# Stationary columns of the chunk steps laid side by side, and their zero matmuls taken out

## The chip, the cores and the metric

The kernel runs on one core of one Trainium2 chip. The metric is the device time of one execution in microseconds (us). A core has TensorE (PE; its weight loads are shown apart as PEld), VectorE (DVE), ScalarE (ACT), GpSimd (POOL), and SyncE (SP), which here only issues transfers. All transfers run on 16 DMA engines. The clock granted to TensorE varies; the profile gives it as a share of full speed.

## The reference

Three stages follow each other: a recurrent attention with a state per head, a mixture of 8 experts with one expert per token, and a gated layer for all tokens. The change is in the first:

```python
B, H, S, D = (4, 8, 768, 48)
k_n = k / (norm(k) + 1e-06)
state = zeros((B, H, D, D))
for t in range(S):
    kt, vt, bt = (k_n[:, :, t], v[:, :, t], beta[:, :, t, None])
    y[:, :, t] = einsum('bhd,bhde->bhe', q[:, :, t], state)
    v_old = einsum('bhde,bhd->bhe', state, kt)
    state = state + bt[:, :, :, None] * einsum('bhd,bhe->bhde', kt, vt - v_old)
```

The output y, 3072 tokens of 384 numbers, goes into the experts (`_moe_ref`: argmax of a gate, two matrices with a ReLU between, scaling) and then into `sigmoid(x @ w_gate) * (x @ w_val) @ w_out`.

## The kernel before

**Chunks and steps.** The 768 tokens of a sequence are cut into 24 chunks of 32. One chunk step `s` does 32 tokens of all 4 batches and 8 heads: the 128 partitions hold 4 batches x 32 tokens. Steps are numbered 0 to 23; `g = s // 4` is the group of four steps, `u = s // 2` the pair of steps, `s2 = s % 2`. Within a chunk the recurrence is solved with the inverse of a 32x32 triangular matrix per batch and head, made for a whole group of four steps at a time.

**One step** (the loop over `s` that begins at line 758), with the names under which the profile shows its parts:

- `KS`: the keys (stationary `KB`) times the state `SH`, 32 matmuls. VectorE makes `W` from it and the values (line 789).
- `Y`, first part: the queries (`QB`) times the state, 32 matmuls. From step 19 on, 12 of these come later in the step.
- zero matmuls into unused columns of U's bank (line 813): 4 a step, 2 from step 19 on. `zf` is a tile of zeros; nobody reads their result.
- `U`: the inverse (`TBD`) times `W`, 32 matmuls. ScalarE rounds U to f16 (`UH[:, 0]`), VectorE takes the remainder (`UH[:, 1]`), so that two f16 halves stand for one f32.
- `XTP`: three transposes of the previous step's output rows, for the gate.
- `GP`: the products of keys with keys and queries of the step 11 chunks ahead, 24 matmuls, with 8 more at the end of the step. Steps 13 to 23 have none left; in their place stand 10 zero matmuls, 2 from step 19 on (line 842).
- `Sps`: the state's update, 48 matmuls (line 858): 2 batch pairs `p`, 3 passes over the f16 halves, 8 heads. The stationary operand is a slice of `KBD`. ScalarE copies the sum to `SH` for the next step.
- `Y`, second part: 24 matmuls (line 866) with a slice of `PBD` as the stationary operand, 3 passes and 8 heads. ScalarE copies Y out (`XG`).
- `GL`: the gate's logits, 12 matmuls.

Step 0 has no KS and no first part of Y; behind its Sps stand 16 more zero matmuls (`BP`, line 861), and ahead of the KS of step 1 stand 8 (`BURST`, line 785).

**KBD and PBD.** Both are block-diagonal over the batches, double-buffered by `u`, zeroed once, and refilled by transfers within SBUF. KBD holds the normalised keys by tokens in two f16 halves, `[128, s2, half, batch of the pair, 64, 8 heads]`: the columns of one head stand 8 elements, 16 bytes, apart. PBD holds the masked products of queries and keys in two f16 halves, `[128, half, 4 batches, 32 tokens x 16]`, where the 16 are 2 steps x 8 heads: the columns of one head stand 16 elements, 32 bytes, apart.

**What fills them.** For PBD: `gp_evac` (line 271) copies the query half of GP to `P` on ScalarE; `p_split` (284) scales and masks on GpSimd; `p_split_hi` and `p_split_lo` make the two halves `PHL`; `expand` (301) issues four transfers of 32 partitions each. For groups ahead of the loop `p_first` and `p_evac` (252, 265) do the same with the tile `PM`. For KBD: `load_kth` reads the keys to `kth`, `kh_mul` (306) scales them on ScalarE, `kh_split_hi` and `kh_split_lo` (316, 323) make the halves `KH` on ScalarE and GpSimd, and `kexp` (329) issues four transfers. In an even step `s`, `expand` and `kexp` for the next pair are issued behind the KS of that step; the tiles are first read two steps later.

**What sets the order.** Each engine's instructions in this stage go out in the order of the program text (class `Queue`, line 95 in the profile stands for all of them). VectorE's work on the next group's inverse is put between its W and UH by `Filler`, by fixed budgets a step (`TA`, `TB`); at the end of a group's fourth step what remains of it is issued in one go. All transfers named here are issued by SP, in program order.

Of the kernel before, what the change touches and what calls it, by code (L numbers as in the profile page):

```python
# [47 lines left out]
WG = 2.7  # L48
WP = 4.5
WE = 1.0  # L50
NU = 4
TC = 3.8
NR = 8
Q2 = 0.0
GS = 6
BURST = {1: 8}
BP = {0: 16}
KA = 1
SHE = (0, 32, 24, 20, 20, 20)
NP = 0  # L60
TA = 2.4
TB = 4.2
W0 = 36
# [15 lines left out]
RK = LA + 1
STROWS = 128  # L80
# [68 lines left out]
class Attention:  # L149
# [5 lines left out]
    def run(self, small, acc, zero_fill, small_loads):  # L155
        tc, a, beside = self.tc, self.a, self.beside
        nc = tc.nc
        V, A, G = [Queue(tc, e) for e in (nc.vector, nc.scalar, nc.gpsimd)]
        T, SP = Queue(tc, nc.tensor), Queue(tc, nc.sync)
        engines = (V, A, G, T, SP)  # L160
        ctx, early = ExitStack(), ExitStack()
        wk = ctx.enter_context(tc.tile_pool(name="at_w", bufs=1, side="right"))
        cp = ctx.enter_context(tc.tile_pool(name="at_c", bufs=1, side="right"))
# [4 lines left out]
        pp = ctx.enter_context(tc.tile_pool(name="at_p", bufs=1, space=PSUM))  # L168
# [9 lines left out]
        KB = [(ep if i < 8 else cp).tile([128, 2, 64, 8], F32, name=f"KB{i}") for i in range(RK)]  # L178
        QB = [cp.tile([128, 2, 64, 8], F32, name=f"QB{i}") for i in range(2)]
        TBD = [(cp if i else ep).tile([128, 2, 1024], F32, name=f"TBD{i}") for i in range(2)]  # L180
        PBD = [cp.tile([128, 2, 4, 512], F16, name=f"PBD{i}") for i in range(2)]
        KBD = [cp.tile([128, 2, 2, 2, 64, 8], F16, name=f"KBD{i}") for i in range(2)]
        Sps = [pp.tile([128, 512], F32, name=f"Sps{i}") for i in range(2)]
        KT, VT, KTOK, KHG, GPM, PHL, LT = {}, {}, {}, {}, {}, {}, {}

# [59 lines left out]
        QF, PM, PP = {}, {}, {}  # L245
# [6 lines left out]
        def p_first(s):  # L252

            u, s2 = divmod(s, 2)
            q = QF[s]
            if s2 == 0:
                PM[u] = wk.tile([128, 32, 16], F32, tag="PHL", name="PM", bufs=4)
            tag = ("GP", "XTP", "GL", "U")[s]
            ps = pool(tag).tile([128, 8, 64], F32, tag=tag, name="P0", bufs=1)
            for h in range(8):  # L260
                for p in range(2):
                    T.matmul(out=ps[64 * p : 64 * p + 64, h, 0:32], lhsT=KB[s][0:112, p, :, h], rhs=q[0:112, p, :, h], start=True, stop=True)
            PP[s] = ps

        def p_evac(s):
            u, s2 = divmod(s, 2)
            ps = PP.pop(s)
            for h in range(8):
                A.activation(out=PM[u][:, :, 8 * s2 + h], in_=ps[:, h, 0:32], func=AF.Copy, scale=rnt[:, 0, 8 * s + h : 8 * s + h + 1])

        def gp_evac(s):

            ps = GPS.pop(s)
            KT.pop(s)
            g, s4 = divmod(s, 4)
            if s4 == 0 and g > 0:
                GPM[g] = [ep.tile([128, 32, 32], F32, tag=n, name=n, bufs=b) for n, b in (("G", 2), ("P", 2))]
            A.copy(out=GPM[g][0][:, 8 * s4 : 8 * s4 + 8], in_=ps[:, :, 0:32])
            return A.copy(out=GPM[g][1][:, :, 8 * s4 : 8 * s4 + 8].rearrange("p i h -> p h i"), in_=ps[:, :, 32:64]).ins


        PMS = {}
# [1 line left out]
        def p_split(u):  # L284
            g, i = divmod(u, 2)
            if g:
                pm = GPM[g][1][:, :, 16 * i : 16 * i + 16]
                G.tensor_tensor(out=pm, in0=pm, in1=rnt[:, g, 16 * i : 16 * i + 16].unsqueeze(1).to_broadcast([128, 32, 16]), op=ALU.mult)
            else:
                pm = PM.pop(u)  # L290
            G.tensor_tensor(out=pm, in0=pm, in1=mask.unsqueeze(2).to_broadcast([128, 32, 16]), op=ALU.mult)
            PHL[u] = wk.tile([128, 2, 32, 16], F16, tag="PHL", name="PHL", bufs=4)
            PMS[u] = pm

        def p_split_hi(u):
# [4 lines left out]

        def expand(dst, src):
            for b in range(4):
                SP.dma_start(out=dst[32 * b : 32 * b + 32, :, b], in_=src[32 * b : 32 * b + 32].rearrange("p a i k -> p a (i k)"))


        def kh_mul(u, half=None):
            r = rnt[:, u // 2].rearrange("p (s h) -> p s h", s=4)
            for i in (range(2) if half is None else (half,)):
# [4 lines left out]
                    continue  # L313
                G.tensor_tensor(out=kt, in0=kt, in1=r[:, 2 * (u % 2) + i].unsqueeze(1).to_broadcast([128, 48, 8]), op=ALU.mult)

        def kh_split_hi(u):
            KH = wk.tile([128, 2, 2, 384], F16, tag="KH", name="KH", bufs=1)
            src = KTOK[u].rearrange("p s d h -> p s (d h)")
            for s in range(2):
                A.copy(out=KH[:, s, 0], in_=src[:, s])  # L320
            KHG[u] = KH

        def kh_split_lo(u):
            KH = KHG[u]
            src = KTOK.pop(u).rearrange("p s d h -> p s (d h)")
            for s in range(2):
                G.tensor_tensor(out=KH[:, s, 1], in0=src[:, s], in1=KH[:, s, 0], op=ALU.subtract)

        def kexp(u):
            KH = KHG.pop(u)  # L330
            for b in range(4):
                SP.dma_start(
                    out=KBD[u % 2][32 * b : 32 * b + 32, :, :, b % 2, 0:48].rearrange("p s a d h -> p (s a) (d h)"),
                    in_=KH[32 * b : 32 * b + 32].rearrange("p s a x -> p (s a) x"))


        def prep(g):
# [416 lines left out]
        mm = lambda **kw: T.matmul(skip_group_check=True, **kw)  # L754
# [3 lines left out]
        for s in range(NSTEP):  # L758
            g, s4 = divmod(s, 4)
# [22 lines left out]
            if s > 0:  # L782
                KSf = pp.tile([128, 512], F32, tag="KS", name="KS")
                KSp = KSf[:, 0:384].rearrange("p (h e) -> p h e", h=8)
                for _ in range(BURST.get(s, N1)):
                    mm(out=KSf[:, 384:512], lhsT=zf, rhs=zf, start=True, stop=True)
                for h, p, r in hp:
                    mm(out=KSp[r, h], lhsT=KB[s % RK][:, p, :, h], rhs=S0[:, p, 48 * h : 48 * h + 48], start=True, stop=True)
                V.scalar_tensor_tensor(out=W, in0=vp, scalar=SIG * KSC, in1=KSp, op0=ALU.mult, op1=ALU.subtract)
# [20 lines left out]
            if s == 0:  # L810
                for _ in range(B0):
                    mm(out=Uf[:, 384:512], lhsT=zl, rhs=zl, start=True, stop=True)
            for _ in range((NUL if s >= LS else NU) if s else 0):
                mm(out=Uf[:, 384:512], lhsT=zf, rhs=zf, start=True, stop=True)
            for h, p, r in hp:
                mm(out=Up[r, h], lhsT=TBD[g % 2][r].rearrange("p b k -> p (b k)")[:, 8 * s4 + h :: 32], rhs=W[r, h], start=True, stop=True)
            fil.run(TA if s else Q2)
# [714 lines left out]
```

## Time and profile before

| | |
|---|---|
| runs | 1119.1, 1122.11, 1122.72 us |
| median | 1122.11 us |
| the profiled execution | 1119.2 us, span 1117.5 us |
| instructions | 22890 |
| packets moved | 73535, 100.13 MB |
| mean granted clock | 0.862 |

The chunk steps take the stretch from about 62 to 392 us of the span; the experts follow to about 655 us, then the gated layer. The page shows busy time per engine, the span in 40 slices, DMA queues and groups of instructions. Nearly all instructions of the chunk steps carry line 95, the helper that records them, so they are read by the names of tiles: `Sps<-UH,KBD` is a matmul into Sps with UH and KBD as operands. Matmuls overlap: the duration of one reaches well beyond the start of the next, so that the cost of a group is read from start to start.

### The profile page before, as it was taken

How to read it: one execution, taken by the hardware profiler on the slowest of the kernel's cores; microseconds unless marked ns; L12 is line 12 of the kernel's file. 1: busy time of each engine (PE TensorE's matmuls, PEld its weight loads, DVE VectorE, ACT ScalarE, POOL GpSimd, SP SyncE). 2: the span in 40 equal slices, each digit the busy share in tenths (PEclk: the TensorE clock that was granted, in tenths of full speed). 3: DMA queues.
4: the chain of work that ended last, by engine and by line, in shares of the span. 5: the costliest groups of instructions: out<-in, count | busy, mean ns of one | idle time of the engine just before them, and what ended most of it. 6: DMA issues, size and time to landing. Idle time of an engine off the chain costs nothing. (4 is left out here: it accounts for less than half of the span.)

```text
span 1117.5 us, 22890 instructions
## 1 busy us (share of the span) xinstructions
PE 1086.5 (97%) x9287; PEld 986.8 (88%) x9288; DVE 552.1 (49%) x1376; ACT 412.5 (37%) x892; POOL 422.4 (38%) x460
## 2 busy tenths in 40 slices
PE   9899999999999999999989999999999999999997
PEld 8798999999999998888888988888888888888886
DVE  7977677877873357756767255430210201201111
ACT  6644545445444245454445422221211211211111
POOL 8544445544642123535544413432131221312312
PEclk8885556755556589999999999999999999999999
DMA  7986634432334336545553322100000000000000
GB/s 188 235 209 158 156 103 129 116 100 75 89 91 137 94 104 217 154 144 185 160 167 110 110 45 71 57 29 1 1 29 1 13 17 1 29 1 1 29 1 28
DMA packets 73535, 100.13 MB, mean 90 GB/s; under 512 B 9721, under 2 KB 62914, under 8 KB 73426
## 3 DMA queue, kind: packets, MB, share of 16 engines
q1 hardware_dynamic: 70354, 89.17, 29.1%
q0 software_dynamic: 3072, 9.46, 2.3%
q8 instruction: 74, 1.21, 0.5%
q14 instruction: 35, 0.29, 0.1%
HBM read 74.94 MB, written 15.80 MB: 81 GB/s over the span
## 5 line engine op out<-in xcount | busy, mean ns | idle before, releaser
L1453 DVE TENSOR_TENSOR gf<-gf,g 128x512 f32<-128x512 f32 x72 | 49.5, 688 | 308.7 <-PE g L1445 308.2
L954 POOL TENSOR_TENSOR gsl<-gf,gsh 128x512 fp32r<-128x512 f32 x68 | 88.4, 1301 | 268.0 <-ACT gsh L953 268.0
L1452 ACT ACTIVATE gf<-g 128x512 f32<-128x512 f32 x72 | 43.0, 597 | 183.4 <-PE g L1445 182.9
L953 ACT CAST gsh<-gf 128x512 fp32r<-128x512 f32 x69 | 42.8, 620 | 146.4 <-DVE gf L1453 146.0
L95 DVE TENSOR_TENSOR X<-X,tmp 128x60 f32<-128x60 f32 (+25 forms) x282 | 91.3, 349 | 1.2
L95 DVE TENSOR_TENSOR tmp<-X,Lt 128x60 f32<-128x60 f32 (+25 forms) x282 | 87.0, 335 | 1.9
L1419 PE MATMUL o<-woh,gsl 128*128 128x384 f32 x272 | 87.2, 338 | 0.0
L1419 PE MATMUL o<-wol,gsh 128*128 128x384 f32 x272 | 86.5, 337 | 0.0
L95 PE MATMUL Sps<-UH,KBD 64*128 64x48 f16 x1104 | 65.4, 228 | 2.6 <-DVE UH L95 2.6
L95 PEld LDWEIGHTS <-KBD 64*128 64x128 f16 x1104 | 62.7, 166 | 5.9 <-issue 4.2
L1134 DVE SCALAR_TENSOR_TENSOR hl<-h,hh 128x460 fp32r<-128x460 f32 (+7 forms) x57 | 33.1, 581 | 65.4 <-ACT hh L1133 65.1
L1445 PE MATMUL g<-yl,wgh 128*128 128x512 f32 x216 | 62.6, 395 | 0.0
L1093 PE MATMUL y<-hh,w2h 128*128 128x460 f32 (+6 forms) x168 | 61.0, 363 | 1.5 <-ACT hh L1133 1.4
L1445 PE MATMUL g<-yl,wvh 128*128 128x512 f32 x216 | 62.3, 395 | 0.0
L1419 PE MATMUL o<-woh,gsh 128*128 128x384 f32 x272 | 61.7, 337 | 0.0
L1445 PE MATMUL g<-yh,wgh 128*128 128x512 f32 x180 | 60.9, 395 | 0.0
L1093 PE MATMUL y<-hh,w2l 128*128 128x460 f32 (+6 forms) x168 | 58.9, 351 | 0.0
L95 ACT ACTIVATE kth<-kth,rnt 128x48 f32<-128x48 f32 x192 | 54.7, 375 | 6.6 <-DMA kth<-in_ktok_dram 6.4
L1419 PEld LDWEIGHTS o<-woh,gsh 128*128 128x128 f32 x272 | 49.7, 188 | 5.8
L95 PE MATMUL GP<-KT,KB 112*64 112x64 f32 x640 | 47.7, 315 | 5.8 <-DMA KB<-in_st_dram 3.7
L1071 POOL TENSOR_TENSOR w1l<-w1r,w1h 128x768 fp32r<-128x768 f32 x19 | 37.1, 1952 | 41.5 <-ACT w1h L1066 41.2
L1419 PEld LDWEIGHTS o<-wol,gsh 128*128 128x128 f32 x272 | 50.6, 188 | 2.4
(333 smaller groups left out, 2559.5 us busy)
## 6 DMA issues: line engine op xcount, KB each, us to landing
w1r<-in_w_dram SPq DMA_DIRECT2D x32, 384.0 KB
w2r<-in_w_dram SPq DMA_DIRECT2D x32, 384.0 KB
KT<-in_st_dram SPq DMA_DIRECT2D x20, 448.0 KB
disp<-TBD SPq DMA_DIRECT2D x8, 772.0 KB
kth<-in_ktok_dram SPq DMA_DIRECT2D x12, 384.0 KB
VT<-in_vtok_dram SPq DMA_DIRECT2D x12, 384.0 KB
KBD<-KH SPq DMA_DIRECT2D x48, 96.0 KB
XG<-in_m2g_dram SPq DMA_DIRECT2D x12, 384.0 KB
```

Source lines behind the costliest of these rows:

```text
L95: r = f(*args, **kw)
L953: (act or nc.scalar).copy(out=hi, in_=src)
L954: eng.tensor_tensor(out=lo, in0=src, in1=hi, op=ALU.subtract)
L1071: engine.tensor_tensor(out=l, in0=self.raw[b][i], in1=h, op=ALU.subtract)
L1093: self.T.matmul(out=ys[c][:, 0:n], lhsT=w2[l][:, f % 2, 128 * c : 128 * c + 128], rhs=(hh, hl)[r], start=(f == 0 and i == 0), stop=(f == 7 ...
L1134: self.V.scalar_tensor_tensor(out=hl, in0=hp[:, 0:n], scalar=0.0, in1=hh, op0=ALU.max, op1=ALU.subtract)
L1419: T.matmul(out=ops_[m][:, 0:384], lhsT=gh[l][:, 128 * m : 128 * m + 128], rhs=wo[r][:, f], start=(f == 0 and i == 0), stop=(f == 11 and i ...
L1445: T.matmul(out=ps, lhsT=gv[w][l][:, c, 128 * f : 128 * f + 128], rhs=Y[r][c], start=(i == 0 and c == 0), stop=(i == 2 and c == 2))
L1452: A.activation(out=gf, in_=gps[0], func=AF.Sigmoid)
L1453: V.tensor_tensor(out=gf, in0=gf, in1=gps[1], op=ALU.mult)
```

## The change

KBD becomes `[128, s2, half, 8 heads, 2 batches, 64]` and PBD `[128, half, 16, 4 batches, 32]`: the 128 columns of one head lie side by side. What feeds them follows: P, PM and PHL hold the 16 ahead of the 32 tokens, KH the heads ahead of the 48; the casts and subtractions of KH read `kth` through a view with heads first, and the copy from GP to P no longer turns the two. The transfers of `expand` and `kexp` place runs of 32 and of 48 f16 numbers. The zero matmuls of the chunk steps are left out, those ahead of the loop and in step 0 ahead of U stay.

```diff
-        PBD = [cp.tile([128, 2, 4, 512], F16, name=f"PBD{i}") for i in range(2)]
-        KBD = [cp.tile([128, 2, 2, 2, 64, 8], F16, name=f"KBD{i}") for i in range(2)]
+        PBD = [cp.tile([128, 2, 16, 4, 32], F16, name=f"PBD{i}") for i in range(2)]
+        KBD = [cp.tile([128, 2, 2, 8, 2, 64], F16, name=f"KBD{i}") for i in range(2)]
...
-            return A.copy(out=GPM[g][1][:, :, 8 * s4 : 8 * s4 + 8].rearrange("p i h -> p h i"), in_=ps[:, :, 32:64]).ins
+            return A.copy(out=GPM[g][1][:, 8 * s4 : 8 * s4 + 8], in_=ps[:, :, 32:64]).ins
...
-            PHL[u] = wk.tile([128, 2, 32, 16], F16, tag="PHL", name="PHL", bufs=4)
+            PHL[u] = wk.tile([128, 2, 16, 32], F16, tag="PHL", name="PHL", bufs=4)
...
-                SP.dma_start(out=dst[32 * b : 32 * b + 32, :, b], in_=src[32 * b : 32 * b + 32].rearrange("p a i k -> p a (i k)"))
+                SP.dma_start(out=dst[32 * b : 32 * b + 32, :, :, b].rearrange("p a k i -> p (a k) i"), in_=src[32 * b : 32 * b + 32].rearrange("p a k i -> p (a k) i"))
...
-                A.copy(out=KH[:, s, 0], in_=src[:, s])
+                A.copy(out=KH[:, s, 0], in_=by_head(KTOK[u][:, s]))
...
-                G.tensor_tensor(out=KH[:, s, 1], in0=src[:, s], in1=KH[:, s, 0], op=ALU.subtract)
+                G.tensor_tensor(out=KH[:, s, 1], in0=by_head(src[:, s]), in1=KH[:, s, 0], op=ALU.subtract)
...
-                    out=KBD[u % 2][32 * b : 32 * b + 32, :, :, b % 2, 0:48].rearrange("p s a d h -> p (s a) (d h)"),
-                    in_=KH[32 * b : 32 * b + 32].rearrange("p s a x -> p (s a) x"))
+                    out=KBD[u % 2][32 * b : 32 * b + 32, :, :, :, b % 2, 0:48].rearrange("p s a h d -> p (s a h) d"),
+                    in_=KH[32 * b : 32 * b + 32].rearrange("p s a h d -> p (s a h) d"))
...
-                for _ in range(BURST.get(s, N1)):
-                    mm(out=KSf[:, 384:512], lhsT=zf, rhs=zf, start=True, stop=True)
...
-            for _ in range((NUL if s >= LS else NU) if s else 0):
-                mm(out=Uf[:, 384:512], lhsT=zf, rhs=zf, start=True, stop=True)
...
-                for _ in range(N2 if s < LS else N2L):
-                    mm(out=GPf[:, 0:128], lhsT=zf, rhs=zf, start=True, stop=True)
...
-                            mm(out=Sps[p][:, 48 * h : 48 * h + 48], lhsT=KBD[u % 2][64 * p : 64 * p + 64, s2, l].rearrange("p a d h -> p (a d h)")[:, h::8], rhs=UH[64 * p : 64 * p + 64, r, h], start=False, stop=False)
+                            mm(out=Sps[p][:, 48 * h : 48 * h + 48], lhsT=KBD[u % 2][64 * p : 64 * p + 64, s2, l, h].rearrange("p b d -> p (b d)"), rhs=UH[64 * p : 64 * p + 64, r, h], start=False, stop=False)
...
-            for _ in range(BP.get(s, NP)):
-                mm(out=Uf[:, 384:512], lhsT=zf, rhs=zf, start=True, stop=True)
...
-                    mm(out=Yp[:, h], lhsT=PBD[u % 2][:, l].rearrange("p b k -> p (b k)")[:, 8 * s2 + h :: 16], rhs=UH[:, r, h], start=(s == 0 and h == 0 and i == 0), stop=(i == 2))
+                    mm(out=Yp[:, h], lhsT=PBD[u % 2][:, l, 8 * s2 + h].rearrange("p b i -> p (b i)"), rhs=UH[:, r, h], start=(s == 0 and h == 0 and i == 0), stop=(i == 2))
```

More of the change, by code (lines that the diff above doesn't have):

```diff
@@ L50 @@
 WE = 1.0
-NU = 4
 TC = 3.8
@@ L55 @@
 GS = 6
-BURST = {1: 8}
-BP = {0: 16}
 KA = 1
 SHE = (0, 32, 24, 20, 20, 20)
-NP = 0
 TA = 2.4
@@ L69 @@
 NY = 10
-NUL = 2
-N2L = 2
 SP2 = 1
@@ L75 @@
 DV = (1, 4, 7, 10, 13)
-N1 = 0
-N2 = 10
 E0, E1 = 256, 256
@@ L256, in p_first @@
             if s2 == 0:
-                PM[u] = wk.tile([128, 32, 16], F32, tag="PHL", name="PM", bufs=4)
+                PM[u] = wk.tile([128, 16, 32], F32, tag="PHL", name="PM", bufs=4)
             tag = ("GP", "XTP", "GL", "U")[s]
@@ L268, in p_evac @@
             for h in range(8):
-                A.activation(out=PM[u][:, :, 8 * s2 + h], in_=ps[:, h, 0:32], func=AF.Copy, scale=rnt[:, 0, 8 * s + h : 8 * s + h + 1])
+                A.activation(out=PM[u][:, 8 * s2 + h], in_=ps[:, h, 0:32], func=AF.Copy, scale=rnt[:, 0, 8 * s + h : 8 * s + h + 1])
         def gp_evac(s):
@@ L286, in p_split @@
             if g:
-                pm = GPM[g][1][:, :, 16 * i : 16 * i + 16]
-                G.tensor_tensor(out=pm, in0=pm, in1=rnt[:, g, 16 * i : 16 * i + 16].unsqueeze(1).to_broadcast([128, 32, 16]), op=ALU.mult)
+                pm = GPM[g][1][:, 16 * i : 16 * i + 16]
+                G.tensor_tensor(out=pm, in0=pm, in1=rnt[:, g, 16 * i : 16 * i + 16].unsqueeze(2).to_broadcast([128, 16, 32]), op=ALU.mult)
             else:
                 pm = PM.pop(u)
-            G.tensor_tensor(out=pm, in0=pm, in1=mask.unsqueeze(2).to_broadcast([128, 32, 16]), op=ALU.mult)
-            PHL[u] = wk.tile([128, 2, 32, 16], F16, tag="PHL", name="PHL", bufs=4)
+            G.tensor_tensor(out=pm, in0=pm, in1=mask.unsqueeze(1).to_broadcast([128, 16, 32]), op=ALU.mult)
+            PHL[u] = wk.tile([128, 2, 16, 32], F16, tag="PHL", name="PHL", bufs=4)
             PMS[u] = pm
@@ L314, in kh_mul @@
                 G.tensor_tensor(out=kt, in0=kt, in1=r[:, 2 * (u % 2) + i].unsqueeze(1).to_broadcast([128, 48, 8]), op=ALU.mult)
+        by_head = lambda x: x.rearrange("p d h -> p h d")
         def kh_split_hi(u):
-            KH = wk.tile([128, 2, 2, 384], F16, tag="KH", name="KH", bufs=1)
-            src = KTOK[u].rearrange("p s d h -> p s (d h)")
+            KH = wk.tile([128, 2, 2, 8, 48], F16, tag="KH", name="KH", bufs=1)
             for s in range(2):
-                A.copy(out=KH[:, s, 0], in_=src[:, s])
+                A.copy(out=KH[:, s, 0], in_=by_head(KTOK[u][:, s]))
             KHG[u] = KH
         def kh_split_lo(u):
-            KH = KHG[u]
-            src = KTOK.pop(u).rearrange("p s d h -> p s (d h)")
+            KH, src = KHG[u], KTOK.pop(u)
             for s in range(2):
-                G.tensor_tensor(out=KH[:, s, 1], in0=src[:, s], in1=KH[:, s, 0], op=ALU.subtract)
+                G.tensor_tensor(out=KH[:, s, 1], in0=by_head(src[:, s]), in1=KH[:, s, 0], op=ALU.subtract)
         def kexp(u):
@@ L838, in run @@
             else:
-                GPf = pp.tile([128, 512], F32, tag="GP", name="GP", bufs=1)
                 for h, p, r in hp[ny:]:
                     mm(out=Yp[r, h], lhsT=QB[s % 2][:, p, :, h], rhs=S0[:, p, 48 * h : 48 * h + 48], start=(h == 0), stop=False)
-                for _ in range(N2 if s < LS else N2L):
-                    mm(out=GPf[:, 0:128], lhsT=zf, rhs=zf, start=True, stop=True)
             if last:
```

## The prediction

> **What bounds the kernel now.** I read the busy shares and the 40 slices first, then the waits of the engines inside the chunk steps, then TensorE's timeline of one step.
>
> ```profile
> PE 1086.5 (97%) x9287; PEld 986.8 (88%) x9288; DVE 552.1 (49%) x1376; ACT 412.5 (37%) x892; POOL 422.4 (38%) x460
> ...
> PEclk8885556755556589999999999999999999999999
> ...
> PE Sps L95 <- DVE UH L95: 2.6, 1, 2.6
> PE U L95 <- DVE W L95: 0.9, 1, 0.9
> ...
> 68.00:392.00 324.00, 320.14 (x4801) 300.63 (x4799) 224.73 (x724) 146.61 (x375) 141.12 (x200) 0.57 0.44 117
> ```
>
> The 24 chunk steps lie between about 62 and 392 us. In that stretch TensorE waited for VectorE twice (columns: us in total, times, longest), 3.5 us, and was busy 320.14 of 324 us at a mean granted clock of 0.57; VectorE was busy 224.73 us (the last row: window, its length, busy us and count of TensorE, its weight loads, VectorE, ScalarE and GpSimd, then granted clock, DMA share, GB/s). So TensorE's own queue, in program order, sets the pace: an interval taken out of it shortens the step, until another engine is late. Nothing behind 392 us is touched; it moves up as a whole.
>
> One step (s = 4) on TensorE's timeline (start, duration, group), then groups of other places that price the edits, and three windows of TensorE alone (length, busy, clock, DMA):
>
> ```profile
> 118.57 2.10 PE L95 MATMUL KS<-SH,KB 128*64 128x48 f32 x32
> 120.46 2.13 PE L95 MATMUL Y<-SH,QB 128*64 128x48 f32 x32
> 122.52 0.61 PE L95 MATMUL U<-zf 128*128 128x128 f16 x4
> 123.05 2.00 PE L95 MATMUL U<-W,TBD 64*64 64x48 f32 x32
> 124.99 0.90 PE L95 MATMUL XTP<-cst,XG 128*128 128x128 f32 x3
> ...
> 127.50 2.90 PE L95 MATMUL Sps<-UH,KBD 64*128 64x48 f16 x48
> 130.34 1.68 PE L95 MATMUL Y<-UH,PBD 128*128 128x48 f16 x24
> 131.95 0.83 PE L95 MATMUL GL<-wgo,xt 128*64 128x16 f32 x12
> ...
> 185.85 2.90 PE L95 MATMUL Sps<-UH,KBD 64*128 64x48 f16 x48
> 188.69 1.00 PE L95 MATMUL Y<-UH,PBD 128*128 128x48 f16 x13
> ...
> 263.32 0.22 PE L95 MATMUL GL<-g_oh,ones 128*128 128x24 f16 x3
> 263.40 0.19 PE L95 MATMUL GL<-acc,ones 128*128 128x32 f16 x1
> ...
> 59.53 2.00 PE L95 MATMUL Sps<-zf 128*128 128x128 f16 x33
> 61.37 0.61 PE L95 MATMUL U<-zl 128*128 128x128 f16 x8
> ...
> 185.85:188.69 2.84, 2.84 (x51) 0.97 0.94 284
> 59.53:61.37 1.84, 1.84 (x37) 1.00 0.98 340
> 263.27:263.51 0.24, 0.24 (x7) 0.50 0.00 0
> ```
>
> Read starts, not durations: matmuls overlap, and a group's cost is the next group's start minus its own. The step is 14.57 us long (its window stands below). Sps costs 130.34 - 127.50 = 2.84 us for 48 matmuls, 59 ns each; the PBD group (the second Y) 1.61 us for 24, 67 ns each; the four zero matmuls 0.53 us.
>
> **The change, part by part.**
>
> *Faster weight loads.* The Sps at 185.85 ran at a granted clock of 0.97, the one at 127.50 in a step at 0.50 (below): 2.84 us both. What does not follow the clock is not the stream of the 48 moving columns; it is the load of the next stationary columns, which stand 16 bytes apart in KBD and 32 bytes apart in PBD, where it is slower still. A load of 128 f16 columns lying side by side is in the trace too: the three products with `ones` take 263.40 - 263.32 = 0.08 us, 27 ns each, at clock 0.50, with 24, 16 and 8 moving columns. So a packed pair costs the larger of 27 ns for the load and the stream. The stream: 33 zero matmuls of 128 columns take 1.84 us at full clock, 56 ns each, 0.44 ns a column; at half the clock 0.87. For 48 columns that is 21 or 42 ns. I take 42 ns, since 0.57 is near half; the ends are 27 ns (full clock) and 59 to 67 ns (no gain). Per step: Sps 48 x (59 - 42) = 0.82 us, PBD 24 x (67 - 42) = 0.60 us.
>
> [...]
>
> *Zero matmuls.* They wait for nothing and stand in TensorE's queue. Per step 1 to 18 four ahead of U, 0.53 us; in steps 13 to 18 ten more in the place of GP; in steps 19 to 23 two and two:
>
> ```profile
> 270.73 1.27 PE L95 MATMUL GP<-zf 128*128 128x128 f16 x10
> 271.93 0.39 PE L95 MATMUL Sps<-UH,KBD 64*128 64x48 f16 x3
> ...
> 338.68 0.39 PE L95 MATMUL GP<-zf 128*128 128x128 f16 x2
> 339.00 2.51 PE L95 MATMUL Sps<-UH,KBD 64*128 64x48 f16 x48
> 341.44 0.26 PE L95 MATMUL Y<-UH,PBD 128*128 128x48 f16 x1
> ...
> 68.80 1.67 PE L95 MATMUL U<-zf 128*128 128x128 f16 x16
> 70.26 1.66 PE L95 MATMUL Y<-UH,PBD 128*128 128x48 f16 x24
> ```
>
> Ten cost 1.20 us, two 0.32, the 16 behind step 0 1.46; for the 8 ahead of step 1 I take 0.9 by the same rate. If nothing else is late: steps 1 to 12 save 12 x (0.53 + 0.82 + 0.60) = 23.4 us; 13 to 18 6 x 3.15 = 18.9; 19 to 22, where Sps now costs 2.44 us and so gains 0.42, 4 x (0.65 + 0.42 + 0.60) = 6.7; step 0 with both extra groups 3.7; step 23 1.1. Together **53.8 us**.
>
> *What is late next.* VectorE's queue in single steps; step 4, and four of the nine that VectorE fills, the first and the last among them:
>
> ```profile
> 86.65:103.98 17.33, 14.73 (x223) 13.75 (x222) 14.12 (x34) 6.28 (x17) 11.47 (x9) 0.50 0.64 156
> 118.57:133.14 14.57, 14.57 (x224) 13.66 (x222) 9.69 (x39) 7.80 (x20) 9.84 (x20) 0.50 0.76 182
> ...
> 162.70:177.29 14.59, 14.59 (x223) 13.68 (x222) 13.53 (x37) 5.80 (x16) 6.30 (x8) 0.50 0.38 115
> ...
> 219.82:235.14 15.32, 14.43 (x223) 13.57 (x221) 14.60 (x45) 5.91 (x16) 5.92 (x8) 0.61 0.45 123
> ...
> 317.88:331.40 13.52, 13.52 (x200) 12.79 (x199) 11.79 (x46) 5.75 (x17) 8.39 (x14) 0.50 0.41 109
> ```
>
> W and UH stand in VectorE's queue among the columns of the next group's inverse, so a step cannot be shorter than VectorE's busy time plus some 0.5 us in which UH must wait for U. Step 4 has room (9.69 against 12.6). Nine do not: besides these four, steps 6, 10, 14, 15 and 16 are busy 12.8, 12.7, 11.3, 12.0 and 12.1 us. Step 6 is held at 13.3 instead of 12.6, step 7 at 14.0 instead of 12.6, step 10 at 13.2 instead of 12.0, step 11 at 15.1 instead of 13.4, step 14 at 11.8 instead of 10.4, 15 at 12.5 instead of 10.4, 16 at 12.6 instead of 10.3, 18 at 12.3 instead of 10.4; step 2, already led by VectorE, keeps 1 us of its gain. The losses are 0.7 + 1.4 + 1.2 + 1.7 + 1.4 + 2.1 + 2.3 + 1.9 + 1.0 = 13.7 us. So 53.8 - 13.7 = **40 us**.
>
> *Covers that get thinner.* Without the ten zeros only the transposes (0.83 us in the step above) stand between U and Sps; the first half of UH ends on ScalarE about as late, so that gain may shrink by some tenths in each of steps 13 to 18. PBD, GL and GP still cover the copies of Sps to SH.
>
> *Copies and splits.*
>
> ```profile
> L95 ACT COPY P<-GP 128x256 f32<-128x256 f32 x20 | 12.9, 646 | 1.9 <-POOL PHL L95 1.9
> L95 ACT COPY G<-GP 128x256 f32<-128x256 f32 x20 | 7.5, 375 | 11.4 <-PE GP L95 11.4
> L95 ACT CAST KH<-kth 128x384 f16<-128x384 f32 x24 | 10.9, 502 | 0.0
> ```
>
> The copy of P writes in strides now (646 ns) and plainly after (as G, 375 ns): minus 0.27 us a step on ScalarE. The casts of KH read in strides after: between nothing and the same 1.06 ns an element, plus 0.41 us each; I take the latter. One cast a step on the average, so plus 0.14 us a step on an engine busy 5.8 to 7.8 us in the steps above: hidden. GpSimd's KH subtraction may cost nothing or some 0.4 us more by the same rate; only a transfer that is needed two steps later awaits it.
>
> *Transfers.* The runs of `expand` shrink from 1024 to 64 bytes and those of `kexp` from 768 to 96: 4 x 1024 + 4 x 1024 = 8192 packets in two steps, 512 for each of 16 DMA engines, against 768 before.
>
> ```profile
> pf<-perm SPq DMA_DIRECT2D x1, 12.0 KB
> ...
> 657.60:659.80 2.20, 2.20 (x11) 1.76 (x11) 1.92 (x4) 0.69 (x2) 0.00 (x0) 1.00 0.82 14
> 157.10:159.80 2.70, 2.70 (x50) 2.70 (x48) 2.70 (x6) 0.48 (x1) 2.50 (x2) 0.50 0.72 171
> ```
>
> The load of pf moves 12 KB as 3072 runs of 4 bytes, 192 an engine; share 0.82 of 2.20 us is at most 9.4 ns each. The other window holds one `kexp`, 512 packets of 768 bytes, 32 an engine: 0.72 x 2.70 us, at most 61 ns each. For 64 and 96 bytes the ends are 9.4 and 61 ns; I take 13, near the short end. That is 6.7 us per engine in two steps of some 25 us, beside 0.44 of busy share now, and needed a step later than it lands: hidden. SP issues the same number of transfers.
>
> [...] No row here shows a short packet between SBUF tiles.
>
> **The rivals.**
>
> 1. *Packed loads are no faster here.* KS and U, f32 with 64 columns, also come at 59 and 61 ns a pair (1.89 and 1.94 us for 32), so 59 ns could be a floor of every small pair. Against it: 27 ns with `ones`. Then only the zeros go: 53.8 less about 32 leaves 22, and VectorE's caps take some 6: 16 us, **1105 us**.
> 2. *The clock rises.* Sps and PBD would fill TensorE for 3 us without a gap, and where the clock is 1.00 a pair costs 27 ns: 72 x 15 ns = 1.1 us a step more, half of it held by VectorE: 12 us more, **1069 us**. For it: the clock was in full in parts of the stretch (mean 0.57, 0.61 in step 11). Against it: the zeros are gone, which are pure streaming.
> 3. *Transfers become the bound: slower.* At 61 ns a packet, whatever its size, the split tiles take 31 us per engine and two steps, and the rest 0.44 x 29.1 less 3.5 = 9.3: 40.5 us for two steps that take 29.1 now. Eleven pairs: plus 125 us, **1247 us**. It costs as much as it gains from (29.1 - 9.3) / 512 = 39 ns a packet.
> 4. *VectorE holds everything:* its steps stretch as GpSimd's traffic falls closer together; the gain halves, **1100 us**.
>
> **How the numbers follow.** The profiled execution took 1119.2 us (span 1117.5), at the low end of the runs shown (1119.1 to 1122.72, median 1122.11). 1119.2 - 40 is 1079, on the median 1082; I write 1081. Chances: forecast 0.52, rival 2 0.20, rival 1 0.13, rival 4 0.09, rival 3 0.06. The range goes from 5 us below rival 2 (1064) to 3 us above rival 1 (1108). A measurement of this kernel tells 0.3%, 3.4 us, from no change. Faster 0.92 (all but rival 3 and a remnant), same 0.02, slower 0.06.
>
> **What would show it.** Steps 3 to 5 near 12.6 us; Sps near 2.0 us and PBD near 1.0 from start to start; TensorE waiting for W and UH in steps 7, 11 and 15; VectorE's share in the stretch above 0.75. Sps still at 2.8 us speaks for rival 1, at 1.3 for rival 2. A DMA share near 1 and waits of Sps or Y for KBD or PBD speak for rival 3. The forecast is wrong if the packed load costs more than 50 ns, or if the transfers land late.

## The result and the profile after

| | before | after |
|---|---|---|
| median of four runs each | 1121.09 us | 1084.01 us |
| lowest and highest | 1119.1, 1122.72 us | 1079.49, 1087.26 us |
| the profiled execution | 1119.2 us, span 1117.5 us | 1079.49 us, span 1077.8 us |
| mean granted clock | 0.862 | 0.898 |

The ratio is 0.9667 (95% interval 0.9624 to 0.9711), 37 us less; the forecast was 1081 us. The sum came out. Several of its terms did not, and what follows is about those. The two profiled executions, each at the low end of its four runs, lie 39.7 us apart.

From the page of the kernel after: busy time, the granted clock in 40 slices, packets, and the queue of SP's transfers (packets, MB, share of the 16 DMA engines' time).

```profile
PE 1022.6 (95%) x9111; PEld 926.5 (86%) x9112; DVE 569.2 (53%) x1376; ACT 416.9 (39%) x892; POOL 430.2 (40%) x460
...
PEclk8976865566569999999999999999999999999999
...
DMA packets 162622, 100.11 MB, mean 93 GB/s; under 512 B 108025, under 2 KB 152002, under 8 KB 162514
...
q1 hardware_dynamic: 159442, 89.17, 35.8%
```

TensorE's timeline of the kernel after (start, duration, group), first the end of step 3, then that of step 4:

```profile
112.50 1.30 PE L87 MATMUL Sps<-UH,KBD 64*128 64x48 f16 x48
113.74 0.78 PE L87 MATMUL Y<-UH,PBD 128*128 128x48 f16 x24
114.44 0.53 PE L87 MATMUL GL<-wgo,xt 128*64 128x16 f32 x12
...
123.74 1.95 PE L87 MATMUL Sps<-UH,KBD 64*128 64x48 f16 x48
125.62 1.14 PE L87 MATMUL Y<-UH,PBD 128*128 128x48 f16 x24
126.70 0.83 PE L87 MATMUL GL<-wgo,xt 128*64 128x16 f32 x12
```

Sps, 2.84 us before at either clock, is 113.74 - 112.50 = 1.24 us in one step and 1.88 us in the next, PBD 0.70 and 1.08 us; over these stretches the granted clock was 1.00 and 0.50. A pair (a matmul and its weight load) with packed columns follows the clock: from one matmul's start to the next lie 25 ns in some steps and 40 ns in the others (the median of each group), where the strided ones had 60 ns (Sps) and 62 ns (PBD) in every step.

Windows of steps 3 to 11, 12 to 18 and 19 to 22, after and then before (length; busy us and count of TensorE, its loads, VectorE, ScalarE, GpSimd; clock; DMA share; GB/s).

```profile
104.50:218.38 113.88, 110.45 (x1949) 104.06 (x1948) 100.85 (x315) 64.02 (x162) 58.63 (x81) 0.62 0.78 155
218.38:300.65 82.27, 72.85 (x1328) 68.22 (x1326) 77.13 (x232) 48.03 (x120) 54.86 (x86) 0.62 0.51 95
300.65:337.69 37.04, 36.67 (x743) 34.62 (x741) 22.07 (x71) 20.36 (x48) 11.31 (x14) 0.80 0.77 164
```

```profile
103.98:235.14 131.16, 130.27 (x1985) 122.80 (x1984) 99.32 (x322) 62.50 (x162) 57.32 (x81) 0.59 0.50 131
235.14:331.40 96.26, 96.26 (x1415) 90.83 (x1414) 72.70 (x239) 45.54 (x120) 53.21 (x87) 0.50 0.32 87
331.40:380.34 48.94, 48.57 (x759) 44.87 (x758) 18.21 (x55) 20.18 (x48) 12.36 (x18) 0.60 0.48 136
```

The difference of the two spans, stretch by stretch, beside what the terms of the prediction give for the same stretch after its deductions for VectorE:

| stretch | before, us | after, us | gained | predicted |
|---|---|---|---|---|
| ahead of U of step 0 | 61.91 | 65.75 | -3.84 | 0 |
| from there to step 1 | 10.72 | 6.02 | 4.70 | 3.7 |
| steps 1 and 2 | 31.35 | 32.73 | -1.38 | 2.9 |
| steps 3 to 11 | 131.16 | 113.88 | 17.28 | 12.5 |
| steps 12 to 18 | 96.26 | 82.27 | 13.99 | 13.2 |
| steps 19 to 22 | 48.94 | 37.04 | 11.90 | 6.7 |
| step 23 and all behind | 737.14 | 740.09 | -2.95 | 1.1 |
| span | 1117.48 | 1077.78 | 39.70 | 40.1 |

From step 0 to step 22 the chunk steps gave 46.5 us where 39.0 were predicted, although steps 1 and 2 lost; the stretches ahead of them and behind them gave 6.8 us back. In steps 12 to 18 TensorE is busy 72.85 of 82.27 us where it had no gap before. Its waits for VectorE in the stretch of the chunk steps (us in total, times, longest), 3.5 us in all before:

```profile
PE Sps L87 <- DVE UH L87: 12.9, 6, 5.3
...
PE U L87 <- DVE W L87: 8.5, 5, 2.7
```

### The profile page after: what moved, and what is told of

The parts are those of the page before. It is cut to its first block, busy times and chain, and to the rows that moved or that the text cites. A ratio compares the mean times of both kernels' runs of the same rounds, so it can differ in the third digit from the quotient of the medians.

```text
span 1077.8 us, 22538 instructions
## 1 busy us (share of the span) xinstructions
PE 1022.6 (95%) x9111; PEld 926.5 (86%) x9112; DVE 569.2 (53%) x1376; ACT 416.9 (39%) x892; POOL 430.2 (40%) x460
## 3 DMA queue, kind: packets, MB, share of 16 engines
q1 hardware_dynamic: 159442, 89.17, 35.8%
## 5 line engine op out<-in xcount | busy, mean ns | idle before, releaser
L87 DVE TENSOR_TENSOR X<-X,tmp 128x60 f32<-128x60 f32 (+25 forms) x282 | 96.1, 367 | 1.2
L87 DVE TENSOR_TENSOR tmp<-X,Lt 128x60 f32<-128x60 f32 (+25 forms) x282 | 94.7, 362 | 1.9
L87 PE MATMUL U<-W,TBD 64*64 64x48 f32 x768 | 47.9, 292 | 8.5 <-DVE W L87 8.5
L87 PEld LDWEIGHTS GP<-KT,KB 112*64 112x64 f32 x640 | 42.6, 221 | 14.7 <-POOL KH L87 7.1
L87 PEld LDWEIGHTS U<-W,TBD 64*64 64x64 f32 x768 | 44.4, 200 | 10.6 <-DVE W L87 9.2
```

The costliest lines, as they stand in the source:

```text
L87: r = f(*args, **kw)
```

## The experiments

Each ratio is to the kernel before, run beside it on the same chip; half widths of differences are put together from both intervals. Only one execution of each kernel is profiled, and its stretches do not repeat to the microsecond: the kernel after and runs 4 and 5 have the same program from step 3 on, and took 113.9, 117.3 and 117.2 us for steps 3 to 11, 82.3, 82.4 and 85.6 for steps 12 to 18.

**1. The layout alone.** The kernel after with all zero matmuls of the chunk steps back (those behind step 0 are not shown):

```diff
+                for _ in range(BURST.get(s, N1)):
+                    mm(out=KSf[:, 384:512], lhsT=zf, rhs=zf, start=True, stop=True)
...
+            for _ in range((NUL if s >= LS else NU) if s else 0):
+                mm(out=Uf[:, 384:512], lhsT=zf, rhs=zf, start=True, stop=True)
...
+                for _ in range(N2 if s < LS else N2L):
+                    mm(out=GPf[:, 0:128], lhsT=zf, rhs=zf, start=True, stop=True)
```

> The kernel after with the zero matmuls of the chunk steps put back: the new layout alone. Theory (the layout is worth its own part, a packed pair costs 39 ns at half clock): Sps about 1.9 us and PBD about 1.07 us from start to start in a half-clock step, steps 4 and 5 near 13 us, and the time 22 to 27 us below the kernel before (ratio 0.976 to 0.980). Rival (the zeros are the whole effect, the packed columns are no faster once the zeros stand in the queue and the clock stays low): Sps 2.8 us and the time within 4 us of the kernel before.

Measured: 1083.18 us, ratio 0.9669 (0.9641 to 0.9697), as the whole change. Its windows for the same three groups of steps:

```profile
103.48:224.66 121.18, 118.69 (x1986) 110.01 (x1985) 100.39 (x314) 63.91 (x162) 57.72 (x81) 0.51 0.74 148
224.66:302.52 77.86, 74.60 (x1416) 70.11 (x1414) 73.41 (x228) 47.82 (x119) 55.33 (x86) 0.80 0.53 99
302.52:341.46 38.94, 38.57 (x760) 35.53 (x758) 23.39 (x76) 20.84 (x49) 12.75 (x16) 0.82 0.75 163
```

So the layout is worth its part and more (37 us, not 22 to 27), and on top of it the zeros' removal bought nothing that these runs can tell. In the two traces it bought 7.3 us in steps 3 to 11 and 1.9 in 19 to 22, but steps 12 to 18 are 4.4 us *shorter with* the zeros, at a clock of 0.80, and from step 23 to the end the execution with the zeros is 2.7 us shorter too (737.4 against 740.1 us; run 5 shows where).

**2. The zeros alone**, taken out of the kernel before, old layout.

```diff
-            for _ in range((NUL if s >= LS else NU) if s else 0):
-                mm(out=Uf[:, 384:512], lhsT=zf, rhs=zf, start=True, stop=True)
...
-                for _ in range(N2 if s < LS else N2L):
-                    mm(out=GPf[:, 0:128], lhsT=zf, rhs=zf, start=True, stop=True)
```

> The kernel before without the zero matmuls of the chunk steps, old layout. Theory (zeros are plain queue time): 0.53 us less in steps 3 to 12, 1.6 us less in steps 13 to 18, less what VectorE holds in steps 7, 11, 15 and 16: 12 to 17 us below the kernel before (ratio 0.985 to 0.989). With the first run the two parts then sum to about the 37 us of the whole change. Rival (VectorE holds steps 13 to 18 already, so zeros there are free): 4 to 8 us below. Rival (the zeros keep the granted clock down): more than 20 us below, with Sps still 2.84 us and KS below 1.9.

Measured: 1110.64 us, ratio 0.9904 (0.9880 to 0.9928), 10.8 us less by the ratio; a little under the range. Alone the two parts are worth 37.1 + 10.8 = 47.9 us, together 37: some 10 us overlap (plus or minus 6). Its window of steps 12 to 18:

```profile
228.57:319.06 90.49, 84.68 (x1328) 81.32 (x1326) 74.90 (x234) 45.47 (x120) 51.79 (x86) 0.61 0.33 91
```

From U of step 0 to step 23 this trace is 14.4 us shorter than that of the kernel before, within the 12 to 17 expected; behind that it is 5.3 us longer, 2.8 of which lie at the jump behind the experts and just after it (run 5).

**3. KBD alone**, with KH and its transfers; PBD and the zeros as before.

```diff
-        KBD = [cp.tile([128, 2, 2, 2, 64, 8], F16, name=f"KBD{i}") for i in range(2)]
+        KBD = [cp.tile([128, 2, 2, 8, 2, 64], F16, name=f"KBD{i}") for i in range(2)]
```

> The kernel before with KBD alone packed (with KH and its transfers), PBD and the zeros as before. Theory: Sps 1.9 us, PBD still 1.61 us; 22 steps of 0.9 us less some 4 us held by VectorE and 2 us given back ahead of the loop by the 96-byte transfers: 12 to 16 us below the kernel before (ratio 0.986 to 0.989). Rival (Sps is held by UH or by VectorE): Sps 1.9 us but the time within 5 us. In the trace the products of chunk 10 should start 1.5 to 3 us later than in the kernel before (52.6 us), if the small transfers ahead of the loads in SP's queue are what delays them.

Measured: 1100.19 us, ratio 0.9814 (0.9792 to 0.9836), 20.9 us less, more than expected. TensorE's timeline at the end of step 4:

```profile
125.54 1.95 PE L95 MATMUL Sps<-UH,KBD 64*128 64x48 f16 x48
127.42 1.68 PE L95 MATMUL Y<-UH,PBD 128*128 128x48 f16 x24
129.03 0.83 PE L95 MATMUL GL<-wgo,xt 128*64 128x16 f32 x12
```

Sps is 1.88 us, PBD still 1.61 us, in one and the same step: each layout acts on its own group, so that the stride and not the clock makes the 60 ns. The products of chunk 10 (the GP of step 10, made ahead of the loop) began at 54.26 us, 1.7 us later than before, as expected if the small transfers delay their loads.

**4. The loads of chunk 10 earlier.**

```diff
         load_kth(1)
+        ahead(10)
         kexp(0)
...
-        ahead(10)
         gp(10)
```

> The kernel after with the loads of chunk 10 (KT and KB) issued ahead of the first refill of KBD. Theory (the prologue of the kernel after is longer because these loads stand behind 4096 small packets in SP's queue and on the DMA engines): the products of chunk 10 start at 50 to 53 us instead of 56.4, U of step 0 at 60 to 62.5 instead of 65.75, and the time is 3 to 5 us below the kernel after (1075 to 1081 us). Rival (another load or VectorE is late instead: the DMA engines are full from 40 to 65 us whatever the order): U of step 0 stays later than 64 us, or step 3 begins as late as before, and the time is within 1.5 us of the kernel after.

TensorE ahead of step 0, in the kernels before, after and with the loads moved (the bracket: how long it had been idle, and what ended that):

```profile
52.56 2.24 PE L95 MATMUL GP<-KT,KB 112*64 112x64 f32 x32 [3.48 <-DMA KB<-in_st_dram]
...
61.91 1.97 PE L95 MATMUL U<-W,TBD 64*64 64x48 f32 x32
```

```profile
56.38 2.26 PE L87 MATMUL GP<-KT,KB 112*64 112x64 f32 x32 [6.98 <-POOL KH L87]
58.57 6.81 PE L87 MATMUL Sps<-zf 128*128 128x128 f16 x84
...
65.75 1.97 PE L87 MATMUL U<-W,TBD 64*64 64x48 f32 x32
```

```profile
51.93 2.27 PE L87 MATMUL GP<-KT,KB 112*64 112x64 f32 x32 [3.26 <-DMA KB<-in_st_dram]
54.13 5.27 PE L87 MATMUL Sps<-zf 128*128 128x128 f16 x84
...
59.78 2.08 PE L87 MATMUL U<-W,TBD 64*64 64x48 f32 x32
64.05 2.25 PE L87 MATMUL GP<-KT,KB 112*64 112x64 f32 x32 [2.19 <-DMA KB<-in_st_dram]
```

In the second bracket the profile names the GpSimd operation on KH, which happened to end then; in the kernel before and in run 4 the products begin ahead of the end of that operation, so that it is the load that they wait for. With the loads ahead of the small packets the products start 4.5 us earlier than in the kernel after, and 1.8 us earlier than in any other run with the whole layout: this part of the theory is shown. U of step 0 starts 6 us earlier; the other 1.5 us come from the 84 zero matmuls, which took 5.27 us instead of 6.81, at a granted clock of 0.92 instead of 0.70. But the gain is lost again in step 0: TensorE waits 2.2 us for the load of chunk 11 (the last line) and 2.1 us for UH, and step 1 began at 71.42 us against 71.77. Time 1081.69 us, ratio 0.9658 (0.9632 to 0.9683): 1 us better than the change, within its interval, as the rival had it. Whether more is won by moving the other loads too was not tried.

**5. 48 zero matmuls where TensorE is idle.**

```diff
-D = {4: 10, 5: 14, 6: 20, 7: 10, 8: 40, 9: 20, 10: 20, 0: 84}
+D = {4: 10, 5: 14, 6: 20, 7: 10, 8: 40, 9: 20, 10: 68, 0: 84}
```

> The kernel after with 48 more zero matmuls ahead of the products of chunk 10, where TensorE stands idle for 7 us: 96 more TensorE instructions, so that the rest of its stream is shifted by 256 instructions against the kernel before instead of 352. [...] In the chunk steps nothing should change by more than 1 us.

TensorE at the start of the gated layer, in the kernel after and with the 48 (line 1319 is the branch around the block for overflowing experts, the jump meant here):

```profile
615.40 1.40 PE L1429 MATMUL g<-XG,wgh 128*128 128x512 f32 x3 [2.87 <-PEq L1319]
616.59 1.49 PE L1429 MATMUL g<-XG,wgl 128*128 128x512 f32 x3
```

```profile
620.91 0.94 PE L1429 MATMUL g<-XG,wgh 128*128 128x512 f32 x3 [1.19 <-DVEq L1319]
621.68 0.85 PE L1429 MATMUL g<-XG,wgl 128*128 128x512 f32 x3
```

The wait is 1.2 us, as in the kernel before, instead of 2.9, and the first groups come 0.77 us apart, as they did there at a clock of 1.00, instead of 1.19 (a clock of 0.83 over the first 10 us). From there to the end the span is 461.0 us instead of 462.4. Time 1077.12 us where the kernel before took 1117.39: ratio 0.9645 (0.9612 to 0.9678), by ratio 2.5 us less than the kernel after, too few for these intervals. The zeros of the chunk steps are missing here as in the kernel after, so that their absence alone does not make the wait long; that the shift of TensorE's stream does was the author's guess, and the table of the last section has what the runs show of it. That the chunk steps would change by no more than 1 us did not hold: with the same program steps 3 to 11 and 12 to 18 took 3.4 and 3.3 us longer than in the kernel after, at a clock of 0.50 instead of 0.62. The profiled execution was the slowest of its four, 1083.6 us.

**6. Zeros in steps 12 to 18 alone.**

```diff
+            for _ in range(4 if 12 <= s < LS else 0):
+                mm(out=Uf[:, 384:512], lhsT=zf, rhs=zf, start=True, stop=True)
...
+                for _ in range(10 if s < LS else 0):
+                    mm(out=GPf[:, 0:128], lhsT=zf, rhs=zf, start=True, stop=True)
```

> The kernel after with zero matmuls put back in steps 12 to 18 alone (4 ahead of U in 12 to 18, 10 in the place of GP in 13 to 18). Theory (in these steps VectorE sets the pace, and the zeros fill TensorE's waits so that its clock stays up; without them the clock falls and Sps and PBD cost 40 ns a pair instead of 25): granted clock of steps 12 to 18 about 0.8 instead of 0.62, these seven steps take 77 to 79 us together instead of 82.3, steps 3 to 11 stay at 114; time 3 to 6 us below the kernel after (1078 to 1081). Rival (the zeros are plain queue time here as elsewhere): seven steps 86 to 90 us, time 4 to 8 us above the kernel after. Rival (what differed was where VectorE and GpSimd collide, by chance): the clock stays near 0.62, the seven steps within 1.5 us of 82.

```profile
218.92:299.06 80.14, 74.23 (x1416) 70.07 (x1415) 76.28 (x228) 47.86 (x119) 54.77 (x86) 0.83 0.51 95
```

The window of the seven steps: the clock is 0.83, as the theory had it, and 80.1 us lie between the theory's 77 to 79 and the 82 of the third reading. Ratio 0.9656 (0.9625 to 0.9686), the same as the change. In runs 1 and 6 the clock is 0.80 and 0.83 with zeros in these steps, in the kernel after and runs 4 and 5 0.62, 0.65 and 0.50 without; but the kernel before has 0.50 with them. That zeros hold the clock up is therefore not shown, only that they cost nothing here.

**7. Half of the scaling of Lt to VectorE.** `Lt` holds the triangular matrices of a group of four steps, which are scaled and then inverted; from group 2 on GpSimd did all of the scaling.

```diff
-R2 = 0
+R2 = 16
```

> The kernel after with half of the scaling of Lt (groups 2 to 5) moved from GpSimd to VectorE, so that the two GpSimd operations of 1.9 and 2.5 us shrink to about 0.6 us each and VectorE gets two of about 0.6 us more. Theory (VectorE is late because its small operations are held for 1.9 to 2.4 us while a long GpSimd operation runs): the single operations of 1.9 and 2.3 us in steps 6, 10 and 14 disappear, VectorE is done earlier, TensorE's waits for W and UH fall from 21 us to 13 to 17, time 3 to 6 us below the kernel after. Rival (VectorE is late by its own count of work): 1.2 us more work a group, waits the same or longer, time 0 to 4 us above.

VectorE and GpSimd in step 6, after and then with this edit:

```profile
146.91 1.95 POOL L87 TENSOR_TENSOR Lt<-Lt,bx 128x1024 f32<-128x1024 f32 x1 [0.61 <-DVE bx L87]
147.01 1.89 DVE L87 SCALAR_TENSOR_TENSOR nbr<-bx,be 128x32 f32<-128x32 f32 x1
...
149.05 2.46 POOL L87 TENSOR_TENSOR Lt<-Lt,nbr 128x1024 f32<-128x1024 f32 x1 [0.19 <-DVE g_pos L87]
...
149.43 2.34 DVE L87 TENSOR_TENSOR X<-X,tmp 128x231 f32<-128x231 f32 x1
```

```profile
143.50 0.66 POOL L87 TENSOR_TENSOR Lt<-Lt,bx 128x256 f32<-128x256 f32 x1 [0.82 <-DVE bx L87]
143.60 0.61 DVE L87 SCALAR_TENSOR_TENSOR nbr<-bx,be 128x32 f32<-128x32 f32 x1
```

An operation of 32 elements a partition took 1.89 us beside a GpSimd operation that began 0.1 us earlier, and 0.61 us when that one was short; the same operation of group 1, in the kernel after at 84.48 us with none beside it, took 0.17 us. In these rows VectorE is held for as long as the other runs. Step 2 fell from 17.4 to 12.6 us, steps 7 and 11 had no wait. But the time rose: 1089.28 us, ratio 0.9761 (0.9718 to 0.9804). Steps 16 and 20 took 17.4 and 17.3 us, waiting for W up to 7.0 us: what the fixed budgets of `Filler` had left over of the next group's columns was issued in one go ahead of it (so I read it; run 11 tests it). Mechanism right, forecast wrong.

**8. One block of the copy to TBD on ScalarE.**

```diff
-            for E, b in zip((V, V, A, A), range(4)):
+            for E, b in zip((V, A, A, A), range(4)):
```

> The kernel after with one of VectorE's two partition blocks of the copy from XT to TBD moved to ScalarE (five groups, 0.28 and 0.86 us each). Theory (VectorE's own work sets the steps at the ends of the groups): 5 x 1.1 us less of it, time 2 to 5 us below the kernel after. Rival (ScalarE is late with UH or SH instead, or TBD comes later for U): time the same or up to 3 us above.

Measured: 1076.61 us beside 1117.39, ratio 0.9655 (0.9623 to 0.9686), 1.3 us better by ratio: inconclusive.

**9 and 10. The scaling moved for groups 2 and 3 alone; then with 5 and 8.**

```diff
-            R = R0 if g < 2 else R2
+            R = R0 if g < 4 else R2
```

> The kernel after with half of the scaling of Lt moved from GpSimd to VectorE for groups 2 and 3 alone (not 4 and 5). Theory (the run with all four groups gained in steps 2 to 11, where step 2 fell from 17.4 to 12.6 us and steps 7 and 11 had no wait, and lost in steps 12, 16 and 20, where VectorE had columns of groups 4 and 5 left over): step 2 near 12.6 us, step 3 begins at 96 to 98.5 us instead of 104.5, steps 3 to 11 take 105 to 114 us, steps 12 to 18 80 to 86 as in the kernel after; time 6 to 12 us below the kernel after (ratio to the kernel before 0.957 to 0.961). Rival (the gain is given back behind it, since the columns of group 4 then fall into shorter steps): ratio 0.965 to 0.970.

> The run before this one, with the 48 zero matmuls ahead of the loop and the copy to TBD moved to ScalarE in one of four blocks. If the three parts add: 8 us from the scaling, 3 us from the jump, 0 to 2 us from the copy: ratio to the kernel before 0.953 to 0.958. Rival (the parts overlap in VectorE): ratio 0.957 to 0.962. A ratio above 0.9645 says that the parts work against each other.

Ratios 0.9646 (0.9616 to 0.9675) and 0.9627 (0.9601 to 0.9653): in both the rival came nearer, the gain was given back. Run 9 began step 3 at 98.23 us, as expected, and then took 17.9 us for step 11. Run 10 has a wait that neither the kernel before nor the kernel after has: two steps stood until their queries were loaded. Its waits for W and UH by VectorE still come to 14.2 us; the transfers are next.

```profile
PE Y L87 <- DMA QB<-in_st_dram: 3.7, 2, 3.1
```

**11. All four groups, and larger budgets**, with the 48 zeros of run 5 and the copy of run 8.

```diff
-R2 = 0
+R2 = 16
...
-TC = 3.8
+TC = 4.6
...
-TA = 2.4
-TB = 4.2
+TA = 2.8
+TB = 4.8
```

> As the combined kernel, but the scaling moved for all four groups and the budgets by which VectorE's columns are spread over the steps raised by 14 to 21 per cent (TA 2.4 to 2.8, TB 4.2 to 4.8, TC 3.8 to 4.6). Theory (what the run with all four groups lost, it lost because the budgets left columns for the end of the group): no wait above 3 us for W in steps 16 and 20, ratio 0.950 to 0.957. Rival (columns of groups 4 and 5 are held by GpSimd's own columns, or VectorE is full there): waits of 5 us and more for W in steps 16 or 20 stay, ratio 0.958 to 0.970; or the larger budgets hold UH back in other steps.

Measured: 1077.30 us beside 1122.72, ratio 0.9595 (0.9571 to 0.9619), the best of all: 0.7% (0.2 to 1.2%) below the kernel after. This is all four edits together; against run 10 the ratio is 0.0032 lower with a half width of 0.0035, so that the budgets' own part is not shown in the time. In the trace it is: steps 16 and 20 have no wait for W. Its waits:

```profile
PE Sps L87 <- DVE UH L87: 7.6, 4, 3.1
PE U L87 <- DVE W L87: 5.6, 3, 2.4
PE Sps L87 <- ACT UH L87: 2.6, 2, 1.8
```

13.2 us for VectorE instead of 21.4. The ratio lies at the low end of the rival's range: its first sign is not there, but its second is, since W is now late in step 14 and UH in steps 15 and 16.

**12. The same with the zeros back**, and without the 48.

> As the kernel with larger budgets, but with all zero matmuls of the chunk steps put back (and without the 48 ahead of the loop, so that TensorE's instruction count is that of the kernel before and the jump behind the experts is short in both). Theory (on top of the new layout the zeros cost nothing only because VectorE set the pace; where VectorE's work is spread, TensorE's queue counts again): 6 to 12 us slower than the kernel with larger budgets, ratio to the kernel before 0.965 to 0.970. Rival (the zeros pay for themselves in any case, by keeping TensorE busy and its clock up): ratio 0.957 to 0.962, as with larger budgets and no zeros (0.9595), with a granted clock above 0.75 in steps 12 to 18.

Measured: 1087.88 us beside 1121.58, ratio 0.9681 (0.9659 to 0.9703): 9.6 us (plus or minus 3.7) slower than run 11. Windows of run 12, steps 3 to 11, 12 to 18 and 19 to 22:

```profile
98.37:216.46 118.09, 116.60 (x1985) 108.28 (x1985) 103.26 (x364) 67.56 (x169) 55.00 (x80) 0.56 0.80 157
216.46:303.38 86.92, 79.30 (x1416) 74.33 (x1415) 67.89 (x235) 50.34 (x125) 50.87 (x86) 0.70 0.50 92
303.38:345.12 41.74, 39.84 (x759) 36.31 (x758) 14.31 (x39) 20.59 (x47) 13.26 (x18) 0.79 0.72 168
```

Run 11 took 112.53, 86.56 and 36.96 us for them, at clocks of 0.64, 0.50 and 0.80. Where TensorE sets the pace the steps with zeros are longer (by 5.6 and 4.8 us, 3.1 of the latter in step 22 alone, where TensorE also stood 1.5 us for no reason that the profile shows); in steps 12 to 18, still held by VectorE in both, they differ by 0.4 us. By the time the theory holds; the stretches agree with it, as far as two traces at different clocks can tell.

## Why the prediction was right, and where it was not

- **What bounds.** TensorE's queue did, until shortened; then VectorE in some of the steps, as forecast: step 7 13.83 us (14.0 predicted), step 11 14.84 (15.1), with waits for W in both, and steps 1, 2 and 14 to 18. In the others TensorE hardly waits, and their length goes with its clock: steps 3 to 5, forecast near 12.6 us, took 10.86, 12.52 and 11.21, the first and third with 25 ns between the matmuls of Sps and the second with 40.
- **Strided loads** cost what was read off, and packing removes it (runs 1 and 3). The size was off: 42 ns a pair were taken, and 40 at half and 25 at full clock measured. The rival of the rising clock was true in part (0.62 in steps 3 to 18, 0.80 in 19 to 22, where 11.9 us came instead of 6.7). The first rival fell: in the same shapes strided pairs took 60 and 62 ns and packed ones 40 and 25, and in run 3 both stand in one step.
- **Zero matmuls.** The term that failed. About 22 of the 53.8 us were theirs, less what VectorE holds; alone they gave 10.8, on top of the layout nothing measurable (run 1). The two parts overlap, and by the traces in steps 12 to 18: there the layout alone gained 18.4 us, the zeros alone 5.8, both together 14.0, while in every other stretch of the table the gains of runs 1 and 2 add up to that of the change within 2.6 us. (The clock there was 0.80 in run 1 and 0.62 after, so that a part of this may be the clock's.) The step of the sum that was wrong is the cap by VectorE: the deductions, 13.7 us, were worked out from its busy time before, but its 1376 operations took 569.2 us after instead of 552.1 (77.13 in steps 12 to 18 against 72.70; step 15 took 16.1 us where 12.5 was forecast). The stretch still came near its forecast, because steps 12, 14 and 18, with 25 ns between the matmuls of Sps, were 1.6 to 2.2 us shorter than forecast. That VectorE's work stretches is the mechanism of the fourth rival, at a smaller size; run 7 shows for single operations that GpSimd holds them (1.89 us beside one of 1.95, 0.61 beside one of 0.66), and that this makes the whole of the difference is argued. Run 12 supports that zeros are queue time where VectorE is not in the way.
- **Steps 1 and 2.** Step 2 was to gain 0.95 us and gained nothing (17.33 and 17.36 us), step 1 grew from 14.02 to 15.37. In step 2 it is VectorE again, held by the long GpSimd operations (with them shortened in run 7 the step took 12.6 us). In step 1 TensorE waits 2.7 us for W, and still 2.8 in run 7: VectorE too, but what holds it there stays open.
- **Transfers: "needed a step later than it lands: hidden".** True in the chunk steps, where no matmul of the kernel after waits for KBD, PBD or QB. False ahead of them. There the DMA engines are full in either kernel (from 36 us to U of step 0 the share is 1.01 before and 1.04 after), and in SP's queue the four transfers of `kexp(0)` stand ahead of the loads of chunk 10. SP's rows for those four, before and after (start, time to issue), and its queue on the page of the kernel before:

```profile
40.59 4.88 SPq L95 DMA_DIRECT2D KBD<-KH  x4
```

```profile
41.93 7.91 SPq L87 DMA_DIRECT2D KBD<-KH  x4
```

```profile
q1 hardware_dynamic: 70354, 89.17, 29.1%
```

The products of chunk 10 began at 53.7 to 56.4 us in all runs with the whole layout and this order, at 52.6 and 52.9 with the old layout, and at 51.93 in run 4: up to the 3.84 us of the table. The price of a packet was about right: the queue's share rose from 29.1% of 1117.5 us to 35.8% of 1077.8 for 89088 more packets, 16 x (385.9 - 325.2) / 89088 = 10.9 ns each, after what the large ones that went had cost; the records of the packets of 64 and 96 bytes themselves last 14.1 and 15.2 ns on the mean. 13 had been taken, and the third rival, which needed 39 to eat up the gain, was far off.
- **"Nothing behind 392 us is touched; it moves up as a whole."** Wrong by some 3 us: with 176 matmuls and their loads left out, 352 of TensorE's instructions, the jump behind the experts costs 1.7 us more (a wait of 2.9 us instead of 1.2), and the gated layer, begun at a clock of 0.83 instead of 1.00 over its first 10 us, another 1.6; with 48 matmuls added ahead of the loop neither is there (run 5).
- **Copies.** As worked out: the casts of KH rose from 502 to 904 ns, the copies of P fell from 652 to 377, hidden on ScalarE:

```profile
L87 ACT CAST KH<-kth 128x384 f16<-128x384 f32 x20 | 17.1, 904 | 0.0
L87 ACT COPY P<-GP 128x256 f32<-128x256 f32 x13 | 4.9, 377 | 3.0 <-POOL PHL L87 3.0
```

So the mechanism of the weight loads was right, but 1081 came out because a larger gain there (25 ns at full clock) made up for the zeros, the prologue and the jump. That these cancelled to 3 us was luck.

## What to carry to other kernels

Lay a matmul's stationary columns side by side when the moving side is short: here, with 48 moving columns, the pair took 40 ns at half clock and 25 at full, where the strided one took 60 and 62 at either. Sum two edits of one queue only up to the engine that is next, and test each alone: here the layout brought more than its price and the zeros less, and together about a fifth of the two was gone. After such an edit, re-tune what fixed budgets were set for the old step length (run 11 did, among other edits), and look at the places far behind, jumps above all.

## What was not expected of the hardware

- A VectorE operation on 32 elements a partition lasts 1.89 us beside a GpSimd operation of 1.95, 0.61 beside one of 0.66, and 0.17 with none. What makes it so, no trace here shows.
- The wait at the jump behind the experts falls into two groups, by the count of TensorE's matmuls: in the fourteen traces it is

| matmuls | traces | wait at the jump, us |
|---|---|---|
| 9287 | before, runs 1, 3, 12 | 1.2, 1.2, 1.2, 0.9 |
| 9159 | runs 5, 10, 11 | 1.2, 1.2, 0.9 |
| 9111 | after, runs 2, 4, 7, 8, 9 | 2.9, 2.5, 3.0, 2.9, 2.8, 2.9 |
| 9199 | run 6 | 2.6 |

  With either layout the same count has about the same wait (9287 before and in run 1, 9111 after and in run 2). What it is about these four counts that makes the wait short or long, no run shows. After the longer wait the gated layer began at a lower clock (0.83 or 0.84 over its first 10 us) in six of the seven traces, and at full clock in run 7.
- The four runs after took 1079.5, 1086.1, 1081.9 and 1087.3 us at granted clocks of 0.898, 0.872, 0.888 and 0.879, a spread of 0.7% where the kernel before had 0.3%. Packed pairs follow the clock (25 and 40 ns), which would explain it; but in runs 1, 8 and 10 the time did not go with the clock, and beside runs 5 to 11 the kernel before spread by 0.5% itself. What sets the clock in the chunk steps stays open.
